# The last layer's wo products with wo moving in four column tiles, in pieces, under a newly searched order

## Chip, cores, metric

One core of one Trainium2 chip. The metric is the device time of one execution in microseconds; medians are of several executions. The record marks every run quoted here as fast: none fell in the slower state that the chip sometimes shows.

## The reference, cut to what matters

Two rounds of cached attention and an MLP over 8 sequences of one token each:

```python
W = min(4096, max(256, Sk // 4))                  # 1024 of 4096 cached positions
q = (x @ wq) in 32 heads of 128
scores = einsum(q, k[:, :, Sk - W:]) * 128 ** -0.5
o = einsum(softmax(scores), v[:, :, Sk - W:])
attention = o.reshape(B, 1, 32 * 128) @ wo        # wo: 4096 x 640
x = x + attention(layernorm(x)); x = x + mlp(layernorm(x))     # twice, same weights
```

What has to be read from memory is the caches' window and the weights; half of each sequence's cache stays in SBUF between the layers, half is read twice. In all that is 216 MB.

## The kernel before

SBUF holds the weights and 26 buffers ("units") of 4096 bytes per partition, into which SyncE's queue loads two heads of K or V at a time (512 KB, 128 rows of 4096 bytes). Every engine's instruction order comes from a searched string, ORDER. What the argument touches:

```python
P, NB, D, H, Q = 128, 8, 640, 32, 160
const = ...tile_pool(name="const"); wpool = ...; unitp = ...; state = ...   # laid out in SBUF in this order
units = [unitp.tile([P, UNIT], BF16, name=f"unit{i}") for i in range(NUNIT)]   # UNIT = 2048, NUNIT = 26
wq_sb = wpool.tile([P, NKC, H * DH], BF16, name="wq_sb")        # then wo_sb, w1_sb, w2_sb
ident = const.tile(...); ones_f = ...; nhalf = ...; ind = ...
mask_u = const.tile([P, 2], FP32, name="mask_u")
# ... (cut)
def load(which, job, i):
    s = take()                                    # a free unit, first freed first
    nc.sync.dma_start(units[s][:], cache[job.b, h0:h0 + 2, SK - W:, :].rearrange(
        "u (m c) d -> m u (c d)", c=TOK))
# ... (cut)
def gather(h0, h1):                               # last layer: heads h0 to h1 through wo, all 8 sequences
    ...
    for h in range(h0, h1):
        for n in range(NKC):                      # wo stationary, 8 columns move
            nc.tensor.matmul(a_ps[0][:, n, :], lhsT=wo_sb[:, h, n * P:(n + 1) * P], rhs=qo[:, :, h],
                             start=first, stop=(h == 2 * JOB - 1), skip_group_check=True)
            first = False
# ... (cut) the resident job's 16 heads, in one block when that job is done:
plan.add(PE, 2.2, lambda: gather(2 * JOB, H), after=[l1k[b].done], rank=1 << 20, take="att", code=160)
# ... (cut) after the searched part:
warm = units[free.pop()][:, 0:2].bitcast(FP32)
nc.scalar.activation(warm, ones_f[:], ACT.Sqrt)
nc.vector.tensor_tensor(out=xT[:, 0, 0:NKC], in0=xT[:, 0, 0:NKC], in1=a_ps[0][:], op=ALU.add)
# ... then the closing layer norm and MLP
```

The softmax here doesn't subtract the row's maximum and nothing guards it: scores larger than these inputs give would overflow.

## Time and profile before

| | before |
|---|---|
| time, median | 569.04 us (568.35 to 569.16) |
| span of the profiled run | 567.0 us |
| first transfer, last packet of the cache loads | 1.7, 547.5 us |
| closing add of the attention (xT) | 555.03 us |
| TensorE, VectorE busy | 399.2, 337.1 us |
| start of the first load buffer in SBUF | byte 117696 = 459 x 256 + 192 |

The last row is not in the profile; it is where the compiled program placed the buffer. At the time of the prediction I had not looked at it. The other rows read as follows: the loads run almost without a break to 547.5 us, and what follows is a chain of small steps. The prediction shows the lines.

### The profile page before, as it was taken

The numbers are of one execution on the slowest core, as the hardware profiler recorded it, in microseconds if no ns is written. First come the engines' busy times: TensorE is split into PE (matmuls) and PEld (weight loads), VectorE is DVE, ScalarE is ACT, GpSimd is POOL, SyncE is SP. The second block draws the span as 40 slices with busy tenths as digits, with TensorE's granted clock in tenths as the row PEclk, the third lists the DMA queues.
The fourth block names the chain that finished last, engine by engine and source line by source line (L and its number), as shares of the span: only waits on it lengthen the run. The fifth ranks groups of instructions, "written<-read, shape, count | busy, mean of one in ns | idle before, by whom it ended". The sixth has DMA issues, their size and how long they took to land.

```text
span 567.0 us, 18836 instructions
## 1 busy us (share of the span) xinstructions
PE 399.2 (70%) x8495; PEld 260.6 (46%) x8495; DVE 337.1 (59%) x665; ACT 78.0 (14%) x195; POOL 11.6 (2%) x24
## 2 busy tenths in 40 slices
PE   2303646886688778677877788777878778878985
PEld 1301434544454455355534564355635454555454
DVE  1148514695747774875568474964479474656732
ACT  0000100121011200210022001210030101210321
POOL 2000000000000000000000000000000000000000
PEclk9999655576556756755556555655575555755765
DMA  8999999999999999999999999999999999999950
GB/s 342 384 410 408 389 373 408 408 409 408 389 398 407 408 403 410 407 408 405 388 401 409 408 405 393 408 408 408 397 395 408 407 400 391 408 406 338 359 232 4
DMA packets 62758, 217.48 MB, mean 384 GB/s; under 512 B 6414, under 2 KB 12246, under 8 KB 62038
## 3 DMA queue, kind: packets, MB, share of 16 engines
q1 hardware_dynamic: 62646, 216.28, 97.2%
q8 instruction: 66, 1.08, 0.8%
q14 instruction: 14, 0.11, 0.1%
q10 hardware_dynamic: 32, 0.01, 0.0%
HBM read 216.25 MB, written 0.01 MB: 381 GB/s over the span
## 4 chain that ended last, share of the span: by engine, by line
DMA 73%; PE 19%; DVE 4%; issue 3%; SPq 1%; ACT 1%
DMA unit_97<-in_A_v_cache_dram 15%; PE s_ps L430 8%; DMA unit_111<-in_A_v_cache_dram 5%; DMA unit_103<-in_A_v_cache_dram 5%; DMA unit_87<-in_A_k_cache_dram 5%; DMA unit_107<-in_A_v_cache_dram 4%; DMA unit_103<-in_A_k_cache_dram 4%; DMA unit_95<-in_A_v_cache_dram 3%; DMA unit_100<-in_A_k_cache_dram 2%; PE qr_ps L681 2%; PE o_ps_142 L482 2%; DMA unit_112<-in_A_v_cache_dram 2%; DMA unit_109<-in_A_k_cache_dram 2%; DMA unit_87<-in_A_v_cache_dram 2%; PE o_ps_141 L482 2%
## 5 line engine op out<-in xcount | busy, mean ns | idle before, releaser
L430 PEld LDWEIGHTS <-qd_154 128*16 128x16 bf16 x512 | 14.7, 108 | 53.1 <-issue 24.1
L540 PEld LDWEIGHTS <-wo_sb 128*128 128x128 bf16 x1280 | 35.6, 103 | 7.6 <-issue 7.4
L540 PE MATMUL att<-ot,wo_sb 128*128 128x1 bf16 x1280 | 36.4, 165 | 3.1 <-DVE ot L531 1.6
L681 PE MATMUL qr_ps<-wq_sb,xn 128*32 128x512 bf16 x320 | 35.8, 609 | 0.4 <-DVE qd_154 L395 0.4
L430 PEld LDWEIGHTS <-qd_155 128*16 128x16 bf16 x512 | 15.3, 111 | 37.7 <-issue 28.6
L395 DVE CAST qd_155<-e_ps 32x64 bf16<-32x64 f32 x64 | 18.2, 285 | 15.1 <-PE e_ps L386 14.3
L430 PE MATMUL s_ps<-unit_93,qd_154 128*16 128x512 bf16 x24 | 10.8, 579 | 19.1 <-DVE qd_154 L395 19.1
L323 PEld LDWEIGHTS <-w_sb 128*128 128x128 bf16 x630 | 17.6, 104 | 10.2 <-issue 5.7
L681 PEld LDWEIGHTS <-xn 128*32 128x32 bf16 x320 | 11.8, 140 | 20.1 <-issue 16.5
L462 ACT CAST p_v<-sh_ps 128x256 bf16<-128x256 f32 x33 | 12.3, 373 | 60.7 <-PE sh_ps L455 60.6
L420 ACT COPY s_ps<-mask_u 128x512 f32<-128x512 f32 x33 | 19.5, 594 | 0.0
L395 DVE CAST qd_154<-e_ps 32x64 bf16<-32x64 f32 x64 | 18.3, 285 | 1.9 <-PE e_ps L386 1.2
L284 POOL TENSOR_TENSOR ln_w<-ln_w,nhalf 128x1 f32<-128x1 f32 x16 | 8.6, 540 | 506.7 <-DVE ln_w L276 407.1
L323 PE MATMUL h_ps<-yT,w_sb 128*128 128x1 bf16 x560 | 16.1, 165 | 4.0 <-DVE yT L289 4.0
L430 PE MATMUL s_ps<-unit_90,qd_155 128*16 128x512 bf16 x40 | 18.2, 594 | 0.8 <-DVE qd_155 L395 0.8
L356 PEld LDWEIGHTS <-w_sb 128*128 128x128 bf16 x560 | 15.8, 104 | 6.1 <-issue 1.3
L470 DVE RECIPROCAL rd<-d_ps 128x16 f32<-128x16 f32 x33 | 7.8, 238 | 18.1 <-PE d_ps L466 18.0
L414 DVE STREAM_TRANSPOSE unit_94<-unit_94 128x1024 uint32<-128x1024 uint32 x10 | 12.3, 1231 | 8.5 <-DMA unit_94<-in_A_k_cache_dram 8.4
L414 DVE STREAM_TRANSPOSE unit_92<-unit_92 128x1024 uint32<-128x1024 uint32 x10 | 12.3, 1227 | 8.4 <-DMA unit_92<-in_A_k_cache_dram 8.4
L430 PE MATMUL s_ps<-unit_108,qd_155 128*16 128x512 bf16 x36 | 16.3, 595 | 0.0
L414 DVE STREAM_TRANSPOSE unit_88<-unit_88 128x1024 uint32<-128x1024 uint32 x7 | 8.7, 1244 | 12.4 <-DMA unit_88<-in_A_k_cache_dram 12.4
L338 ACT ACTIVATE th<-hu 128x14 f32<-128x14 f32 x8 | 1.7, 215 | 104.0 <-DVE hu L333 104.0
(578 smaller groups left out, 1223.9 us busy)
## 6 DMA issues: line engine op xcount, KB each, us to landing
unit_97<-in_A_v_cache_dram SPq DMA_DIRECT2D x14, 512.0 KB, 10.3
unit_108<-in_A_k_cache_dram SPq DMA_DIRECT2D x11, 512.0 KB, 8.9
wq_sb<-in_A_wq_dram SPq DMA_DIRECT2D x5, 1024.0 KB, 9.9
wo_sb<-in_A_wo_dram SPq DMA_DIRECT2D x2, 2560.0 KB, 16.1
unit_90<-in_A_k_cache_dram SPq DMA_DIRECT2D x10, 512.0 KB, 9.2
unit_94<-in_A_k_cache_dram SPq DMA_DIRECT2D x10, 512.0 KB, 10.3
unit_100<-in_A_k_cache_dram SPq DMA_DIRECT2D x10, 512.0 KB, 10.3
unit_88<-in_A_v_cache_dram SPq DMA_DIRECT2D x10, 512.0 KB, 10.2
```

The costliest lines, as they stand in the source:

```text
L284: nc.gpsimd.tensor_tensor(out=t["wv"], in0=t["wv"], in1=nhalf[:].to_broadcast([P, nb]), op=ALU.pow)
L323: nc.tensor.matmul(t["h"][:, fc, :], lhsT=w1_sb[:, kc, c0:c0 + P], rhs=t["y"][:, kc, :], start=(kc == 0), stop=(kc == NKC - 1))
L356: nc.tensor.matmul(t["o"][:, n, :], lhsT=w2_sb[:, fc, n * P:(n + 1) * P], rhs=t["g"][:, fc, :], start=(fc == 0), stop=(fc == NFC - 1))
L395: nc.vector.tensor_copy(qd[:, :, 0:3:2, :, i], e)
L414: nc.vector.transpose(t, t)
L420: nc.scalar.copy(job.s_ps[:].rearrange("p (x u) -> p x u", u=2), mask_u[:, None, :].to_broadcast([P, 256, 2]))
L430: nc.tensor.matmul(s_ps[32 * a:32 * a + 16, :].rearrange("p (t c) -> p t c", c=32), lhsT=job.first.qd[:, je, o:o + 16], rhs=k[:, je // 2, ...
L462: nc.scalar.copy(job.p_v[:], job.sh_ps[:])
L470: nc.vector.reciprocal(job.rd[:], job.d_ps[:].rearrange("p (a z u) -> p z a u", z=2, u=2))
L482: nc.tensor.matmul(job.o_ps[:, 2 * i:2 * i + 2], lhsT=v[:, c * DH:(c + 1) * DH], rhs=job.p_v[:, a, z, c, :], start=(first and c == 0), sto ...
L540: nc.tensor.matmul(att[job.b][:, n:n + 1], lhsT=wo_sb[:, h, n * P:(n + 1) * P], rhs=job.ot[:, hi:hi + 1], start=(h == 0 and n == 0), stop= ...
L681: nc.tensor.matmul(t["qr", g][32 * a:32 * a + 32, :], lhsT=xn[:, kc, :], rhs=wq_sb[:, kc, c0:c0 + 512], start=(kc == 0), stop=(kc == NKC - ...
```

## The change

Its intent: shorten the work after the last load. The wo products of the last layer go with the 8 outputs stationary and wo moving, 320 columns at a time, four column tiles side by side, in pieces of 4 or 8 heads, so that pieces can run under the loads. The result lies as rows, in four partial sums; two copies and six fp32 matmuls against a small 0/1 matrix, sel, sum it and turn it. ORDER is searched anew for this task list.

```diff
-ORDER = ( ... )                       # all of it replaced
+ORDER = ( ... )
+    att_bank = psA.tile([P, 512], FP32, name="att")
...
+    sel = const.tile([P, 2, NB], FP32, name="sel")
+    for z in range(2):
+        nc.vector.tensor_tensor(out=sel[:, z], in0=ident[:, 32 * z:32 * z + NB], in1=ident[:, 32 * z + 64:32 * z + 64 + NB],
+                                op=ALU.add)
...
         for h in range(h0, h1):
-            for n in range(NKC):
-                nc.tensor.matmul(a_ps[0][:, n, :], lhsT=wo_sb[:, h, n * P:(n + 1) * P], rhs=qo[:, :, h], ...)
+            for z in range(2):
+                g = 64 * (h % 2) + 32 * z
+                nc.tensor.matmul(att_bank[g:g + NB, 0:2 * Q], lhsT=qo[:, :, h],
+                                 rhs=wo_sb[:, h, 2 * Q * z:2 * Q * (z + 1)], ...)
...
-        add_job(l1k[b], q2k, [normed], base=base)
-        if b + 1 == NB:
-            plan.add(PE, 2.2, lambda: gather(2 * JOB, H), after=[l1k[b].done], rank=1 << 20, take="att", code=160)
+        add_job(l1k[b], q2k, [normed], base=base, late=late if b + 1 == NB else None)
...
-    nc.vector.tensor_tensor(out=xT[:, 0, 0:NKC], in0=xT[:, 0, 0:NKC], in1=a_ps[0][:], op=ALU.add)
+    rows = units[free.pop()][:, 0:4 * Q].bitcast(FP32)
+    nc.scalar.copy(rows[:, 0:Q], att_bank[:, 0:Q])
+    nc.vector.tensor_copy(rows[:, Q:2 * Q], att_bank[:, Q:2 * Q])
+    a_ps = psC.tile([P, NKC, NB], FP32, tag="c", name="a_ps")
+    n = 0
+    while n < D:                       # 128, 128, 64, 64, 128, 128 columns
+        z, n1 = n // (2 * Q), min((n // P + 1) * P, (n // (2 * Q) + 1) * 2 * Q)
+        nc.tensor.matmul(a_ps[n % P:n % P + n1 - n, n // P, :], lhsT=rows[:, n - 2 * Q * z:n1 - 2 * Q * z],
+                         rhs=sel[:, z], start=True, stop=True)
+        n = n1
+    nc.vector.tensor_tensor(out=xT[:, 0, 0:NKC], in0=xT[:, 0, 0:NKC], in1=a_ps[:], op=ALU.add)
```

One line of it carries more than its intent: sel is 64 bytes per partition in the pool of constants, and everything laid out behind that pool, the weights and the 26 load buffers, moves up by 64 bytes.

More of the change, by code (lines that the diff above doesn't have):

```diff
@@ L45 @@
 ORDER = (
-    "57(CzL4%2#&zHzDzBz?#z@*&%)$:,#z6z:zK8-1z6zG$&zFz2z1z1+,zGzE2zAzAzBz.z.z.{){.{)z=z>z.z.z:%z~z-z8z8*-,"
-    "%zxz4z4z)z3z)+*&#z.z&z/##%$z/z%y}z.z+y}z%z*y|z%y|y|z#y~zYy|y|y|#y{zS##zQyyyyyyyyyyyy##+2$zF3ys+,zBzB"
-    "yqzAzAyq-&yoyoyoz;z;yoz:yo%(ymymymz4z6%z9z:ylz7#$yjzVz<#yjz2z;z1z/yjytyjz*yjz)&yiyiz%yoyhz)z%ynyh/%$"
-    "z#y~y|yj#yi%&(+*yty_y_z-yuybycy_yaylymy_yaz($)yhycyg#-ye*(yX#ysyWyrysyqyW$ypzXy^yny^##y[yWyZyhyhyZyT"
-    "y[yeyT&#ySzFyWyRyVyRySy[#zByRyUyUyWySySyR$yQz7#%yPyRySz2$yMz0yMyOyUyUyUyUz)$(yN%yQ$1y}$y|$/yLyyyzyyy"
@@ L51 @@
-    "LyHyK#yuyJ$ysyIyJyIypypyIyI.yH(yD&yByhyjyDyDyDyDyD&#&#yf&y=yly>yHy^y>y>y;y=y=ydyZ%yBy:y:#y[1y>y8%yZy"
-    "Wy<y7$#yPyPy9yIyNy9y5yH#&yJyeyJy6(y2$y5yA+yCyWy?yAy0y0y;y>y;y=yLy;yMy<y6,y9y9yG+yE+yF(##$y3#y(#$z%y;"
-    "y&z$#y:y%y.y$yzy+$y4y#y/y$y)y0y0y#y&y.yny#y*y%y%%y$y(y$y$&y#x}#yayay.y.y.y^y.(*+*xy#xwy&xyySy%%y$yR%"
-    "yQxzx~x~x~$x}$xyxuxsyExyxuyCxsxw%$#?.xrxrxoxq-xpxpy5xq#xpxpxmxoxoxv,xnxkxsxsy8xky9#8&3y;yU$(xlxlxzxe"
-    "y-)xlxjxj$xixsxcxry&y$%$xf$#x_xmx_xwxkxbx_(#xhxgxtxhx_#xpxhy,y)xlxmx`xg$x]xdxc$$#$x_x^xVx_xqx]xpxpxV"
@@ L56 @@
-    "x]x]xlxW(&#xXxSxSxUxUxVyLxb#$xTyIxS#x]xRxRxRxUxPxWxQ#$xT%#%xLxMxK*xMxM*xIxIxIy.y.y.xV&xUxHy*$xSy(xSx"
-    "HxGxHxPxLx}xO)xNxH&(xyxKxKxD&xIxIxsxI%xpxHxFxGxExFxjxD.CxCxC#xd#xAxB0-xKx@x@x=x?x?x<x>xDxo(x;#xkx:1$"
-    "-%x<x<x_x<#$(xWx9x3xExU.x7xCx9(+xO%$x>xexKx?x5x=xI$x4xF#x;x,x9x_xDxCx>x,xUx9x?)x2x.x<#x8x*x9x5xI#(&("
-    "x(x0x(x1x-#x@x(#x#x)x+x$x+x(x#%x3x&x2xzx3x3$#xtx#w|w~#w}x+x$x*w}x$w}%wzw|)1wywy$#x`$wuwwwuwvx[wux&x&"
-    "x&wuwux$*wvxSw~,w}xNxN&wzw{w{wx)&&wwxEwwwxxFxCxDwwwwww$0wrwtwpx;x;%#-#.#wmwm<wl0wlwlwiwe&wiwiwdwdwgw"
@@ L61 @@
-    "nwgwd#wk&wjwcwywiwbx52+wuwfx/##w^w^x(w^wow^wn-%wx&w]%wux3wxw[w^%0-wpwZwo$wnwbwowYx%x*wawlwkwawWwZw_w"
-    "U#(wT$wSw]#wYw^wXwXwnwSwowRwYwQwTwWxRwT%wSwgwcwSwbwPwa)$wPwQwPxE$%(#wMx?#&wT(wMwKwKwGwLwNx6wH$wLwL#w"
-    "HwFwFwHwHwFx+wFx*$wPwP(%$wM$wC$wzwCwywIw?wHwHwHwuwHwHwH$w>w@wFwA%#wjw<wAwhw=w@w@w@wdwC$0w>&w9w^w<w<#"
-    "0w:&)$w7w5w6w6w4w=.+#w2%w1wew7wHw7w7wYwFwV86w5w.wXw.w5w3w.wPw3wMw2w2wI)&&%,#wC$#w3w%w-w)(&w.w#w%w(w-"
-    "w6w2w+w.w%$w%w+w/)&#w@w$wFuw#$%$pqss$$ssprnw1ow3now-onw*wpnw(w(wmnw&#w%mnpmpn#$(#/ni$wZ$ggfhhfwSffr%"
@@ L66 @@
-    "qqqewM)&nnwGekwEl)kkew@w@#$&g%w<fw:fw9`^w7di^ccc$&$w.(_w,Zw+^#]Zw&w)Yw7$#)WWW`WsW^w%U],#*%vQQn$$j$h#"
-    "eik#.Pff`&(Nfcc]#%L_^GKMVGLG%$(PHODOO##LCKK$BAXCGI&TFBJIIG#AC?B$E>A@@B0#C>SSS>R#Q;>O<<M<$K+J+$H77##E"
-    "55B5A)4?4>$$?2;256$+6663#94=R40/5%131#1-0XEF#.$.-#>$==+&#%JH#8&$66%656==#&$394##$04$3.2#---.-/#%+.%*"
-    "%#()($(&##$#")
+    "zH<?1,(%zIz^)71@.3%&zC)+#)#z5#z5723+z0)zFz0z/z/zL$zHzEz0%%z@z-z,z,z,z,z?z,z,z8z8z8z,z-z~/+*z-z,*z0zx"
+    "zyz0z0zszsz0*z&&-%%$z)zkz+z$z(z##z%z&z*y|z&zez)z(y}z#y|z$y|$$y{zUyz%#zRyxyx/#2$,zMzKysysysysysys(yr-"
@@ new lines @@
+    "yqzAzAyqyqyq++yoz;z;)ynynynz7z7ynynz7ynynzHz6z7z8*%ymylz@z4z3%#z0%yi%yhyh)ygz(ygz2z,z-ymymz&z?#yl#yk"
+    "yeyeyiyiyz$yz&*ybyr#%)%yay^yoyoybyky`yj)0yjy[yhyby{y^y[#yd&%#$yVypyVyry^yVy[y[yky[yVyhyVyVyiyfyfyfzS"
+    "#zNyWyYyYyZy]yWyUy^#$yWyU%yUyT##$ySyO,yNyNyOz6yOz5z3z4yN$yMyXyOyW*z,yNyU$yTyNz&ySySyQz#z%&yQyQ$yPyP$"
+    "yHyJywyN$yIysyGyHyIyI%yHyHyl#yGyG&-+#*)yAyAy?y`y@y_y_y@y^y@y@yH,y?yZ$y>yjyby]yD&(#yay]yb4$y9y>yXy>y>"
+    "y@yU&%#*y5y;y4yNy4y7yLy7yE#y6y3y5y=yAy=yEy3y<y3yWy<y;y;y=y=,*$%%y8*yNy7y5y-#yCy.yBy2y2y2y?y?y2yAy@y?"
@@ new lines @@
+    "#/y<y2#y)y~y0z$y{$$y6y.y.##y-(y$y/%y#x~y(yly+y$y%y%$#y%x~,x{&x{x|yay`x{x}xzy)(*y&y&yVy&y&y&yT)&x}.yO"
+    "yO%#(4yLyKxzxvxyxyxy#yEyExyxxyCxxxxyAxtxwxwxw,xvy;*y<xp$y;*#y=xrxoxm*))(xlxvxl##xiy:xixgxhxhxey($y3x"
+    "dxky1y$y(#$xzy$y&xbx{xhxhxhx|x{xh#xa*%*xqxtxvxtxp#%xa+y*xbxbxZ)+xjxgxXx^#xZx{$.xaxXxa)xTxTxUxnxoxT#%"
+    "xSxX%xgxRxVxixexUxfxexUxU%xP$xOxQxRx[xXxSxRyExO#xV$&#xOxLxKxMxOy5xO$xKxJxLy2xJxJy0y.xJy-xUxUy+,xKxS%"
+    "xKxQ*y##%&xMxMxMx|xyxFxLxL*xKxt%xG%&#xoxFxFxFxFxkxFxFxFxF#xCxexBxD1#xaxaxA$*x^x=%-,x[xFx;x`x;x9x:x:x"
@@ new lines @@
+    "a$x9xax6x>xOx>,x5xL-xSxLx5x:.*(xOxMx7xfxf%%x/x/xHxbxH$$x1x-x0x-#x,x-x.*(x*x=x+xOxOx+x:x9x9xKx6x3x+x1"
+    "*))x.x.x0x0x&)#x-$%%$x&x8)x&w{x4#wz)%xww|w|wx$wzw|x+x*x%x)w}x$xiw~w}wzw|w~xdwzw}wzw|#w{.x_wxwxwux[wu"
+    "xYx%&ww&$w}(xQw|w|w|wq)wzwxxJxJ%$ww#wvwvwpwmwtwmxAws/wnwq#x<wpwpwlx8wowk%)wlwlx2wlwi#-x.x.wjx-$.)%wf"
+    "x(wpwfx(x+%we$wd&wbwbwzw`wgwawy%wew`w~wdw~w~wv$wrwcwqw^##$#wnwm$w_wjw]#wjw[wn$wiwlwhwhwZwZwVwcwewxwe"
+    "%(wTwTw`wUwX&&()(%wk$wVwh$wUwLwLwRwRwawR*wK#wOw[w]wKwJwZ&wXxBwNwWwSwLwO#wSwNwHwJ##x6wN%x4wMwHwHwEwF%"
@@ new lines @@
+    "wHx.wEwG,wDx*wD(x&%wBwMwMwDwLwFw{(wJ)w|wIw?.wGwvwtwtwtwGwEwrwF0*1(.wA(wjw@wAwhw@&#w>wdwd$wBw=wcw=w=#"
+    "w<w:wawa#w^w:w:w:w8%w8w8(w?$w4wZw5w0w2)w2wY&&w-wRw51w.w,wK%$#wJw)w)w)1wDwDw+w+wBw+w>w+w[w(w*#$(w:w3w"
+    "3w9w4w8%%vw%w/&w.w$w-+w&uw+tw<uw;w@w)w##x&($&w#vvw$pup$,$w+w+mw+w)p#ow%lw$ntprwilnrwar%m#%w[kjjk#(hh"
+    "wTwS(grfq((fwKnnnimwFwHmi&kkkccw>%dgw;(&e#b_bb$a_#w/,^w-^[],wA[$*+&*Vu(aUrTqq*SSpSSw)qlolYtw%vrYSX$#"
+    "VlmV%e#$SNeg$S$#)a`[Y,]IXLLXI&SSTS#G#Pa$E#%C#J#AJ#IGGQOGHIGBGF%EEE$DYY##EVVVDU*;AA@$OO?,MM99)&:HH:G:"
@@ L70 @@
+    "FJ7E9$C&(A84?e94:<G<@@<:8#<$8TS89()36$K4$#3&,0VUC00.,?.MM(-#,:G,*,D,%#%$$1$<0*#.##.55#+,%%#/1*$&($**"
+    "#%##%(&#$#$##")
 Q = D // 4
@@ L195, in _kernel @@
     o_banks = [psO.tile([P, 512], FP32, name=f"o_ps{i}") for i in range(2)]
+    att_bank = psA.tile([P, 512], FP32, name="att")
     for i in range(2):
-        for t in (psS.tile([P, 512], FP32, tag="s_ps", name="s_ps"), o_banks[i]):
+        for t in (psS.tile([P, 512], FP32, tag="s_ps", name="s_ps"), (o_banks + [att_bank])[i], (o_banks + [att_bank])[i + 1]):
             nc.tensor.matmul(t[:].rearrange("p (x i) -> p x i", i=P), lhsT=ident[:],
@@ L535, in project @@
         if job.p0 == 0 and h0 == 0:
-            att[job.b] = psA.tile([P, NKC], FP32, tag="att", name="att")
+            att[job.b] = att_bank[:, 0:NKC]
         for hi in range(h0, h1):
@@ L751, in _kernel @@
     free[:] = range(NUNIT)
-    a_ps = []
+    opening = [True]
     def gather(h0, h1):
-        if not a_ps:
-            a_ps.append(psA.tile([P, NKC, NB], FP32, tag="att", name="a_ps"))
-            first = True
-        else:
-            first = False
-        for h in range(h0, h1):
-            for n in range(NKC):
-                nc.tensor.matmul(a_ps[0][:, n, :], lhsT=wo_sb[:, h, n * P:(n + 1) * P], rhs=qo[:, :, h],
-                                 start=first, stop=(h == 2 * JOB - 1), skip_group_check=True)
-                first = False
+        for h in range(h0, h1):
+            for z in range(2):
+                g = 64 * (h % 2) + 32 * z
+                nc.tensor.matmul(att_bank[g:g + NB, 0:2 * Q], lhsT=qo[:, :, h],
+                                 rhs=wo_sb[:, h, 2 * Q * z:2 * Q * (z + 1)],
+                                 start=opening[0] and h < h0 + 2, stop=(h // 2 == JOB - 1), skip_group_check=True)
+        opening[0] = False
     def late(after, h0, h1):
-        return plan.add(PE, 0.14 * (h1 - h0), lambda: gather(h0, h1), after=[after], rank=1 << 20, code=10 * (h1 - h0))
+        return plan.add(PE, 0.135 * (h1 - h0), lambda: gather(h0, h1), after=[after], rank=1 << 20, code=4 * (h1 - h0))
     def add_queries(job, after=()):
```

## The prediction

> **What bounds the kernel now.** I read the page first (busy shares, the 40 slices, the chain), then the chain in order of time over the last 100 us, then a table of windows around the end, then the timeline of the last 30 us, and last the rows of the operations that the change swaps.
>
> The page says that transfers set the pace:
>
> ```profile
> PEclk9999655576556756755556555655575555755765
> DMA  8999999999999999999999999999999999999950
> ...
> HBM read 216.25 MB, written 0.01 MB: 381 GB/s over the span
> ...
> DMA 73%; PE 19%; DVE 4%; issue 3%; SPq 1%; ACT 1%
> ```
>
> The reader is to see that DMA is full in all slices but the last two, and that 73% of the chain is transfers. Where the stream is full it moves 408 GB/s; 216.3 MB at that rate are 530 us. The change removes no byte, so only two places can yield time: holes in the stream, and the tail after the stream. The windows show both (columns: stretch, its length, busy us of PE, PEld, DVE, ACT, POOL with counts, granted clock, DMA share, GB/s):
>
> ```profile
> 510.00:520.00 10.00, 9.03 (x194) 5.62 (x198) 6.89 (x17) 0.90 (x3) 0.54 (x1) 0.50 0.92 309
> 520.00:530.00 10.00, 8.19 (x161) 5.06 (x158) 6.04 (x12) 2.11 (x5) 0.54 (x1) 0.58 1.02 407
> 530.00:540.00 10.00, 8.19 (x146) 4.29 (x144) 8.65 (x17) 3.27 (x9) 0.00 (x0) 0.83 0.93 339
> 540.00:548.00 8.00, 7.18 (x160) 4.32 (x164) 2.21 (x9) 1.64 (x4) 0.00 (x0) 0.63 0.85 339
> 548.00:567.00 19.00, 12.25 (x342) 10.41 (x334) 4.79 (x23) 3.86 (x6) 0.00 (x0) 0.50 0.01 3
> ```
>
> The last load (value rows into unit_98) was issued at 537.7 and took 10.2 us, so the stream ends at 547.9. From 1.6 us, where the first transfer starts, that is 546.3 us for 530 us of bytes: some 16 us of holes, spread over the run (0 to 20 us, 510 to 520, 530 to 540 are the visible ones). The holes are waits of the load queue for TensorE and VectorE to hand a buffer back. After 547.9 come 19.1 us in which no load runs. The chain there:
>
> ```profile
> 546.77 0.59 PE o_ps_142 L482 x16
> 547.36 1.81 PE o_ps_141 L495 x16
> 549.17 0.54 PE d_ps L466 x2
> 549.71 0.40 PE o_ps_142 L482 x16
> ...
> 551.01 0.57 PE o_ps_142 L482 x16
> 551.57 0.22 PE o_ps L517 x8
> 551.79 3.22 PE a_ps L763 x120
> 555.01 0.02 issue
> 555.03 0.21 DVE xT L806
> ```
>
> From 546.8 to 555.0 TensorE is the bound and nearly never idle: values and groups that are behind the stream (about 4.9 us), then 120 of the 160 wo matmuls in one block (3.22 us). From 555.03 to 567 the closing layer norm and MLP run as one chain that the change does not touch.
>
> **What the Trainium skill says.** Four places bear on it. "TensorE: Matmul & The Clock Gate", the section "Wait — 56ns, not 53.3ns?", says that start to start never falls below about 25 ns however few columns move. The trace agrees: 120 matmuls of 8 columns in 3.22 us are 26.8 ns each at a granted clock of 0.50, and the opening's 156 of the same form took 4.24 us, 27.2 ns, at clock 1.00. So the old form costs the same at either clock. The same page, "Back-to-back issue gap", gives N/1.2 ns at the cold clock and N/2.4 warm: 320 columns would be 267 or 133 ns. The trace agrees in kind: the closing y_ps, 56 matmuls of 160 columns in four column tiles, took 2.06 us at 0.50, that is 14 rounds of 147 ns. "TensorEngine Tiling (Array Packing)", "Restrictions and Gotchas", says that column tiling excludes the fast weight load; with 8 columns of weights this costs nothing here (their load of 103 ns in the groups at L495 lies beside the matmuls). "FP8 and Floating Point Precision", "TensorE Precision Notes", counts four passes for true fp32. The trace shows two records of load and matmul for each fp32 matmul, with loads of about 0.31 us:
>
> ```profile
> L466 PE MATMUL d_ps<-rs_9825,ones_f 128*128 128x16 f32 x2 | 0.6, 386 | 0.0
> L266 PE MATMUL st_ps<-xT,ones_f 128*128 128x96 f32 x2 | 0.7, 459 | 0.6 <-DVE xT L262 0.6
> L829 PE MATMUL y_ps<-w_sb,unit_92 128*32 128x160 bf16 x56 | 2.1, 339 | 0.9 <-DVE unit_92 L345 0.9
> L763 PE MATMUL a_ps<-qo,wo_sb 128*128 128x8 bf16 x160 | 4.6, 174 | 0.0
> ```
>
> **The change part by part.** 1. *The wo products.* Before: 32 heads x 5 column blocks = 160 matmuls, wo stationary, 160 x 27 ns = 4.3 us of TensorE. After: 32 heads x 2 halves = 64 matmuls of 320 columns with the 8 queries' outputs stationary, four column tiles at a time, hence 16 rounds. At clock 0.50, which rules from 545 on, a round is 267 to 280 ns: 4.3 to 4.5 us in all; at 1.00 about 2.2 us. So at the end of this kernel the swap by itself is worth nothing; per head it is 135 ns before and 135 to 140 after.
>
> 2. *By pieces.* Before, the 16 heads of the resident job could be added only in one block after that job was wholly done (80 matmuls, 2.1 us); that block, with two late pieces of the other jobs, makes the 120 at the end. After, they go by 8 heads, each ready as soon as its half is finished. What must stay last is a piece of 4 heads: 2 rounds, the last with its latency of about 0.45 us, some 0.73 us in place of 3.35 us: 2.6 us off the path if everything else finds room earlier. There is room: between 539 and 547 TensorE stands idle for about 2 us, waiting for value loads (0.9, 0.45 and 0.55 us are the larger waits). If a piece finds no room it goes on the path at 1.1 us for 8 heads.
>
> 3. *The sum and the turn.* New on the path, after the last piece: a copy out of PSUM of 128x160 on each of two engines side by side (VectorE's copy of that size takes 0.325 us; ScalarE by the slope between its 128x256, 373 ns, and 128x512, 594 ns, about 0.29), then 6 fp32 matmuls with 128, 128, 64, 64, 128 and 128 weight columns. Each is two loads and two matmuls. In d_ps and st_ps two full loads of 0.31 us end 0.50 us after the first began, so they follow each other at 0.19 us. Eight full and four half loads: 8 x 0.19 + 4 x 0.09 = 1.9 us, plus 0.2 us until the last result. With 0.06 us of handing over the addition is 0.33 + 0.06 + 2.1 = 2.5 us. The final add of 0.20 us stays.
>
> 4. *Setup.* Two VectorE operations on 128x8 and two clearing matmuls of 512 columns, under the first weight load: nothing. The bank for att is now held for good; it had one buffer before as well: nothing.
>
> 5. *The order.* Every engine's order is another one from first load to last. This part has no cost that a row of the trace shows. It can close or open holes; 16 us are there to be had, of which the older search left these behind.
>
> Sum: tail -2.6 + 2.5, about 0; some of the 4.9 us backlog ahead of the block may move forward into idle room since the whole end was ordered afresh, which I put at -1 us (half of the 2 us idle); the holes by the new order I put at -0.5 us with a wide spread. That gives -1.5 us on 569.0: 567.5.
>
> **The rivals.** *The summation eats it and more*: if the pieces of the resident job still end up behind the stream, because its last value groups do so today (they run at 547.3 to 549.2), then 12 heads remain last: 6 rounds, 1.8 us, plus 2.5 of summation against 3.35. That makes +1 us: 570. The clock at 0.50 speaks for it. *The new order decides*: a changed sequence of buffer returns moves the stream's end by some us either way. For it speaks that all of the string changed, and that the queue's waits (single ones of up to 5 us) are many; against it, that both orders come from a search with the same aim, and that a stream 97% full has little room. It would give 563 to 572. *The swap is hidden anyway*: the tail's gain and cost cancel and the stream stays as it was: 569, same. *Faster clock*: moving matmuls of 320 columns may bring the granted clock up at the end, which would shorten the closing chain's wide matmuls by up to 1 us; but the groups at L495 (512 columns) ran at 0.50 just there, so I give it little.
>
> **How range and chances follow.** To be 2% faster the kernel would have to reach 557.7, so to find 11.3 us: two thirds of all the holes, or a tail that is more than halved. To be 2% slower it would have to lose 11.4 us, which only a bad order could do. Both get 2 in 100. The range is the order's spread about the centre: 563.5 to 571.5.
>
> **What would show it.** Right: the row of the wo products has 64 matmuls of 320 columns, the last block of them is short (under 1.3 us), two copies and about 2 us of fp32 matmuls stand between it and the add; the time from the last landing to the add shrinks from 7.1 us to 5 to 7 us; the closing chain after the add is 12 us as before; the stream ends within 4 us of 547.9. Wrong: the fp32 matmuls take under 1 us or over 3 (the loads do not follow each other at 0.19 us); the stream's end moves by more than 4 us (then the order, not the wo part, is the change); or 12 and more heads still stand at the end.

## The result, and the profile after

The changed kernel takes 556.55 us (555.75 to 557.04, 4 runs) against 569.1 us of the kernel before in the same rounds: ratio 0.978, 95% interval 0.9763 to 0.9797. Ratios here are the mean time of one kernel's fast runs over that of the other's in the same rounds, so not quite the ratio of the medians quoted. The time lies 7 us under the range that I gave.

The page of the changed kernel, the lines that answer to those in the prediction:

```profile
PEclk7555555575565655585566655675555555755775
DMA  8999999999999999999999999999999999999950
GB/s 337 416 419 409 404 395 399 396 418 417 419 414 417 418 407 406 416 418 416 406 402 418 416 408 411 416 417 417 397 417 418 417 408 414 417 393 368 367 232 4
...
HBM read 216.25 MB, written 0.01 MB: 390 GB/s over the span
...
DMA 67%; PE 22%; DVE 5%; SPq 4%; issue 1%; ACT 1%; ACTq 0%
```

And the line of the page of the kernel before that I did not print in the prediction, the rate by slice:

```profile
GB/s 342 384 410 408 389 373 408 408 409 408 389 398 407 408 403 410 407 408 405 388 401 409 408 405 393 408 408 408 397 395 408 407 400 391 408 406 338 359 232 4
```

The DMA line is the same, digit for digit. But read the rates: before, the full slices stand at 407 to 410 GB/s, and none is above. After, they stand at 416 to 419. The transfers were as busy before as after; they were slower while busy. A stretch where TensorE is all but idle shows it without any hole (columns as in the windows of the prediction). Before:

```profile
24.00:46.00 22.00, 0.60 (x3) 0.10 (x3) 11.60 (x16) 0.00 (x0) 0.00 (x0) 1.00 1.03 409
```

After:

```profile
24.00:46.00 22.00, 0.59 (x1) 0.17 (x2) 7.07 (x13) 0.00 (x0) 0.00 (x0) 0.50 1.03 420
```

TensorE has 0.6 us of work here in both, so nothing that TensorE does can explain 409 against 420 at the same DMA share of 1.03. VectorE differs, 11.60 us busy against 7.07, and the granted clock too. The first two experiments below settle that. The same stretch in before_pad64, the old order with the 64 bytes, and in after_shift, the new order without them:

```profile
24.00:46.00 22.00, 0.60 (x3) 0.18 (x4) 11.94 (x17) 0.00 (x0) 0.00 (x0) 1.00 1.03 420
24.00:46.00 22.00, 0.59 (x1) 0.18 (x2) 6.17 (x12) 0.00 (x0) 0.00 (x0) 1.00 1.03 410
```

So the rate follows neither VectorE nor the clock.

The end of the changed kernel:

```profile
530.00:535.00 5.00, 4.42 (x102) 3.10 (x100) 1.12 (x6) 1.45 (x2) 0.00 (x0) 0.84 0.82 329
535.00:554.00 19.00, 11.52 (x244) 9.50 (x244) 4.16 (x21) 2.28 (x5) 0.00 (x0) 0.50 0.01 3
```

The last packet lands at 534.9 us, 12.6 us sooner than before (547.5), and 19.1 us remain, against 19.5. So the whole gain of 13.0 us of span is in the stream except 0.4 us. Holes (stretches in which the load queue waits for a free buffer) do not explain it: before, 216.28 MB at 408 GB/s are 530.1 us of the 545.8 between first transfer and last packet, 15.7 us of holes; after, at 418 GB/s, 517.4 of 533.2, 15.8 us of holes. By these round rates, of which 1 GB/s is 1.3 us, the new order closed none of them on balance.

The chain of the changed kernel after the last loads (start, length, what):

```profile
535.33 0.58 PE o_ps_142 L487 x16
535.92 0.44 PE o_ps_141 L487 x16
...
536.60 0.99 PE o_ps_141 L487 x32
537.59 1.74 PE att L765 x19
539.33 0.02 issue
539.36 0.30 ACT unit_107 L808
539.66 0.04 issue
539.70 2.31 PE a_ps L814 x12
542.01 0.02 issue
542.03 0.21 DVE xT L817
```

From the last packet to the add it is 7.1 us, against 7.5 before: the last block is shorter (1.74 us for 3.22), and less work stands ahead of it (2.7 us for 4.3), but the copies and the fp32 matmuls (0.30 and 2.31 us) stand behind it.

The trace also holds every packet's duration. Packets of 4096 bytes are the rows of the cache loads, 49152 in each run. Of these:

| 4096-byte packets | before | after |
|---|---|---|
| mean, median | 165.0, 161 ns | 161.8, 159 ns |
| share at 160 ns or less | 45% | 98% |
| mean without the 1% of 200 ns and over | 162.1 ns | 159.1 ns |

3.2 ns on each of 49152 packets, over 16 engines, are 9.8 us; the 1280-byte and 3456-byte packets of the weights (60.3 to 57.5 and 148.6 to 135.3 ns) add 1.5, of which the 3456-byte part is mostly not the address: after_shift, with w1 where it was before, has 138.3 ns. What makes up the rest of the 12.6 us is not shown.

### The profile page after: what moved, and what is told of

Read it like the earlier page. It is cut to its first block, busy times and chain, and to the rows that moved or that the text cites. A ratio compares the mean times of both kernels' runs of the same rounds, so it can differ in the third digit from the quotient of the medians.

```text
span 554.0 us, 18686 instructions
## 1 busy us (share of the span) xinstructions
PE 400.2 (72%) x8413; PEld 260.8 (47%) x8413; DVE 335.5 (61%) x668; ACT 77.6 (14%) x196; POOL 11.6 (2%) x24
## 3 DMA queue, kind: packets, MB, share of 16 engines
q1 hardware_dynamic: 62646, 216.28, 97.5%
## 4 chain that ended last, share of the span: by engine, by line
DMA 67%; PE 22%; DVE 5%; SPq 4%; issue 1%; ACT 1%; ACTq 0%
PE s_ps L435 8%; DMA unit_104<-in_A_v_cache_dram 5%; DMA unit_112<-in_A_k_cache_dram 5%; DMA unit_96<-in_A_v_cache_dram 4%; DMA unit_91<-in_A_v_cache_dram 4%; DMA unit_89<-in_A_k_cache_dram 4%; DMA unit_94<-in_A_v_cache_dram 4%; DMA unit_94<-in_A_k_cache_dram 3%; DMA unit_89<-in_A_v_cache_dram 3%; DMA unit_99<-in_A_v_cache_dram 3%; PE o_ps_141 L487 3%; DMA unit_103<-in_A_v_cache_dram 3%; DMA unit_100<-in_A_v_cache_dram 3%; SPq L408 2%; DMA wq_sb<-in_A_wq_dram 2%; DMA unit_108<-in_A_k_cache_dram 2%
## 5 line engine op out<-in xcount | busy, mean ns | idle before, releaser
L686 PE MATMUL qr_ps<-wq_sb,xn 128*32 128x512 bf16 x320 | 33.9, 580 | 0.9 <-DVE xn L294 0.6
L435 PE MATMUL s_ps<-unit_102,qd_160 128*16 128x512 bf16 x28 | 12.5, 585 | 22.1 <-DVE unit_102 L419 22.1
L419 DVE STREAM_TRANSPOSE unit_102<-unit_102 128x1024 uint32<-128x1024 uint32 x12 | 14.8, 1231 | 15.5 <-DMA unit_102<-in_A_k_cache_dram 15.5
L328 PEld LDWEIGHTS <-w_sb 128*128 128x128 bf16 x630 | 17.5, 104 | 9.6 <-DVE yT L294 6.8
L425 ACT COPY s_ps<-mask_u 128x512 f32<-128x512 f32 x33 | 19.5, 594 | 0.1
L419 DVE STREAM_TRANSPOSE unit_109<-unit_109 128x1024 uint32<-128x1024 uint32 x11 | 13.5, 1229 | 9.4 <-DMA unit_109<-in_A_k_cache_dram 9.4
L419 DVE STREAM_TRANSPOSE unit_100<-unit_100 128x1024 uint32<-128x1024 uint32 x12 | 14.7, 1228 | 6.9 <-DMA unit_100<-in_A_k_cache_dram 6.9
L435 PE MATMUL s_ps<-unit_100,qd_161 128*16 128x512 bf16 x40 | 17.6, 580 | 0.8 <-DVE unit_100 L419 0.8
L435 PE MATMUL s_ps<-unit_94,qd_161 128*16 128x512 bf16 x40 | 18.0, 594 | 0.0
L460 PEld LDWEIGHTS <-ident 128*32 128x32 bf16 x528 | 10.1, 117 | 16.5 <-issue 14.7
L419 DVE STREAM_TRANSPOSE unit_92<-unit_92 128x1024 uint32<-128x1024 uint32 x12 | 14.8, 1231 | 5.0 <-DMA unit_92<-in_A_k_cache_dram 5.0
L435 PE MATMUL s_ps<-unit_92,qd_160 128*16 128x512 bf16 x40 | 17.1, 574 | 0.7 <-DVE hx L333 0.7
```

The costliest lines, as they stand in the source:

```text
L328: nc.tensor.matmul(t["h"][:, fc, :], lhsT=w1_sb[:, kc, c0:c0 + P], rhs=t["y"][:, kc, :], start=(kc == 0), stop=(kc == NKC - 1))
L419: nc.vector.transpose(t, t)
L425: nc.scalar.copy(job.s_ps[:].rearrange("p (x u) -> p x u", u=2), mask_u[:, None, :].to_broadcast([P, 256, 2]))
L435: nc.tensor.matmul(s_ps[32 * a:32 * a + 16, :].rearrange("p (t c) -> p t c", c=32), lhsT=job.first.qd[:, je, o:o + 16], rhs=k[:, je // 2, ...
L460: nc.tensor.matmul(job.sh_ps[32 * i:32 * i + 32, a], lhsT=ident[:, 32 * a:32 * a + 32], rhs=turned[:, :, 0:4, i].rearrange("p t (z u) -> p ...
L686: nc.tensor.matmul(t["qr", g][32 * a:32 * a + 32, :], lhsT=xn[:, kc, :], rhs=wq_sb[:, kc, c0:c0 + 512], start=(kc == 0), stop=(kc == NKC - ...
```

## The experiments

Theory A: the 64 bytes of sel moved the load buffers from 192 past a multiple of 256 bytes onto one (117696 to 117760 = 460 x 256), and that sets the packets' time. Theory B: the new order (another mix of K and V, other loads side by side) did. All runs were correct against the reference. The time of the kernel before in these calls was 568.7 to 569.2 us.

### The 64 bytes alone, and everything but the 64 bytes

The kernel before with the 64 bytes (before_pad64):

```diff
     mask_u = const.tile([P, 2], FP32, name="mask_u")
+    pad = const.tile([P, 16], FP32, name="pad")
+    nc.vector.memset(pad[:], 0.0)
```

> The kernel before with one unused constant of 64 bytes per partition ahead of the weights and the load buffers, so that the load buffers start at 117760 bytes (a multiple of 256) in place of 117696 (192 past one). Same instructions in the same order. Theory A (the start of the load buffers in SBUF sets how long a 4096-byte packet takes): nearly all packets take 159 ns, the stream ends 10 to 13 us sooner, 556 to 559 us. Theory B (the new order made the stream faster): no change, 568 to 570 us.

Measured: 557.67 us (556.04 to 557.89), ratio 0.9796 (0.9772 to 0.9820); 98.5% of the packets at 160 ns or less. Its rates by slice:

```profile
GB/s 335 391 420 418 400 397 417 417 417 419 400 403 416 419 416 411 417 419 413 400 413 419 416 410 396 419 417 418 396 409 417 417 411 403 417 416 341 341 221 4
```

The changed kernel without them (after_shift; sel lives behind the load buffers):

```diff
-    sel = const.tile([P, 2, NB], FP32, name="sel")
+    sel = state.tile([P, 2, NB], FP32, name="sel")
```

> The changed kernel with its constant sel moved behind the load buffers, so that these start at 117696 again, as in the kernel before; everything else, the order too, as changed. Theory A: packets of 161 to 169 ns come back, 567 to 570 us. Theory B: stays at 556 to 557 us.

Measured: 568.75 us (568.00 to 570.30), ratio 1.0002 (0.9994 to 1.0010); 45% of the packets at 160 ns or less. Its rates by slice:

```profile
GB/s 342 408 409 396 398 384 378 393 410 408 406 399 408 407 405 391 408 408 407 397 401 409 408 389 409 407 407 408 391 409 407 408 395 405 407 383 350 370 216 4
```

The full slices of the old order read 416 to 420 with the 64 bytes, those of the new order 407 to 410 without. Theory A holds in both directions, B falls. The 64 bytes move the weights and the tiles behind the buffers as well. These are not what counts: in the compiled after_shift the tiles behind the buffers start where they do in the changed kernel (xT at 224256 in both), and its packets are slow; in before_half, below, the weights start where they do in the kernel before, and most packets are fast.

The second run also gives the value of everything that the change meant to do: nothing, to within 0.1%. With the buffers on the grid in both it is 556.55 us (changed) against 557.67 (before_pad64); the intervals of their ratios, of four runs each, overlap, so a gain of about 1 us there is neither shown nor excluded.

### Which starts are slow

after_pad128 and after_pad32 put 128 and 32 bytes more ahead of the weights of the changed kernel (`pad = const.tile([P, 32], FP32)` and `[P, 8]`, with the same memset), before_off64 puts 128 ahead in the kernel before. after_all256 moves w1 behind the load buffers and pads 128 bytes, so that the buffers start on a multiple of 256 that is not one of 512:

```diff
+    w1pool = ctx.enter_context(tc.tile_pool(name="w1pool", bufs=1))      # right after the units' pool
-    w1_sb = wpool.tile([P, NKC, F], BF16, name="w1_sb")
+    w1_sb = w1pool.tile([P, NKC, F], BF16, name="w1_sb")
+    pad = const.tile([P, 32], FP32, name="pad"); nc.vector.memset(pad[:], 0.0)
```

> The changed kernel with 128 bytes more ahead of the load buffers: they start 128 past a multiple of 256. Theory A in its strict form (the grid is 256 bytes): packets slow again, 566 to 570 us. Theory A with a grid of 128 bytes: 556 to 557 us. Theory B: 556 to 557 us.

> The changed kernel with 32 bytes ahead of the load buffers, so that all start 32 past a multiple of 256. Any start off the grid is slow: 566 to 570 us; grid of 32 bytes: 556 to 557 us.

> The kernel before with 128 unused bytes ahead of the weights: all load buffers start 64 past a multiple of 256. If any start off the grid is slow, 566 to 570 us; if only some are (192 and 128 have been), 557 us.

> The changed kernel with w1 put behind the load buffers and 128 bytes ahead of the weights: weights and load buffers all start on multiples of 256, but the load buffers 256 past a multiple of 512. Grid of 256 bytes: packets stay at 159 ns, the weights' packets too, 555 to 556.5 us (up to 1 us under the changed kernel). Grid of 512 bytes: packets slow, 566 to 569 us.

| run | start of the load buffers past a multiple of 256 | 4096-byte packets at 160 ns or less | time, us | ratio (95%) |
|---|---|---|---|---|
| before | 192 | 45% | 569 | 1 |
| before_pad64 | 0 | 98.5% | 557.67 | 0.9796 (0.9772 to 0.9820) |
| before_off64 | 64 | 44% | 568.72 | 1.0000 (0.9992 to 1.0008) |
| after_shift | 192 | 45% | 568.75 | 1.0002 (0.9994 to 1.0010) |
| after_pad32 | 32 | 39% | 569.28 | 1.0014 (1.0004 to 1.0025) |
| after_pad128 | 128 | 59% | 566.92 | 0.9966 (0.9952 to 0.9980) |
| changed kernel | 0 | 98% | 556.55 | 0.9780 (0.9763 to 0.9797) |
| after_all256 | 0 (256 past 512) | 98% | 555.90 | 0.9774 (0.9753 to 0.9795) |

All four starts off the grid are slow, both starts on it are fast, whichever of the two orders runs. 128 past is a little less slow than the others (2 us); in that run wq, wo and w1 happen to lie on multiples of 256, so part of it may be theirs. Among the starts tried, the grid is 256 bytes, not 128 and not 512.

### How many buffers must be aligned

before_half puts the 64 bytes between the 13th and 14th load buffer of the kernel before, before_gap20 between the 20th and 21st; before_halfrev puts 64 ahead of the weights and 64 between the 13th and 14th, so that the first half is aligned and the second is 64 past.

```diff
-    units = [unitp.tile([P, UNIT], BF16, name=f"unit{i}") for i in range(NUNIT)]
+    units = [unitp.tile([P, UNIT], BF16, name=f"unit{i}") for i in range(13)]          # 20
+    gap = unitp.tile([P, 32], BF16, name="gap"); nc.vector.memset(gap[:], 0.0)
+    units += [unitp.tile([P, UNIT], BF16, name=f"unit{i}") for i in range(13, NUNIT)]  # 20
```

> The kernel before with 64 unused bytes between the 13th and the 14th load buffer: half of the buffers start 192 past a multiple of 256 as before, half on a multiple. Same order. If the start of each buffer sets the time of the packets written to it, half of the gain comes: 562 to 564.5 us, with some 72% of the 4096-byte packets at 159 to 160 ns (before 45%, all aligned 98%). If the gain came from something else that the 64 bytes shift (the weights, the state behind the buffers), it is all or nothing: 557 or 569 us.

> The reverse half: 64 bytes ahead of the weights, so that the first 13 load buffers start on multiples of 256, and 64 bytes between the 13th and 14th, so that the last 13 start 64 past one. If it is the number of misaligned loads in a row, and not which buffers or what lies behind them: as before_half, 558 to 561 us. If the second half alone matters (before_half aligned that one): 567 to 570 us.

> The kernel before with 64 unused bytes between the 20th and 21st load buffer: 20 of 26 buffers (76% of the loads) start 192 past a multiple of 256. In before_half slow packets were rare where one misaligned load followed an aligned one and common from the fifth misaligned load in a row on. Theory queue (the delay builds up over loads in a row and an aligned load lets it drain): weighted by the runs of before_half, some 20% slow packets, 560.5 to 563 us. Theory linear (each misaligned load pays for itself): 566.5 us.

Measured: before_half 559.24 us, 94% of packets at 160 ns or less; before_halfrev 558.82 us, 94% (ratio 0.9834, 0.9819 to 0.9849); before_gap20 563.81 us, 72% (0.9925, 0.9907 to 0.9943). My number for before_half was wrong: half of the alignment gave 1.7% of the 2.0% (ratio 0.9828, 0.9812 to 0.9845). So a misaligned buffer does not simply pay for itself. It is not a matter of which half, since the reverse did the same. I put the packets of these runs to their loads (128 each, in order of their starts; the loads' buffers from the same issue order in the kernel before), and took the share of packets over 160 ns by the place of a load in a row of misaligned ones:

| place in a row of misaligned loads | 1st | 2nd | 3rd | 4th | 5th |
|---|---|---|---|---|---|
| before_half | 3% | 5% | 12% | 24% | 54% |
| before_halfrev | 2% | 5% | 15% | 35% | 41% |
| before_gap20 | 8% | 18% | 38% | 48% | 52% |

So packets get slower over misaligned loads in a row, and aligned loads undo that. (The last column rests on 3, 4 and 25 loads.) The number that I drew from this for before_gap20 (560.5 to 563) was too low and the linear one (566.5) too high: with only 6 aligned buffers the recovery is not complete, as the first column shows (8% where before_half had 3%). That some queue on the write side fills and drains is my reading; no row of the trace shows a queue.

### What the moving form costs, and what the rest is worth

The changed kernel with the old form of the products, in the new pieces and order, added directly (after_oldform):

```diff
-            for z in range(2):
-                g = 64 * (h % 2) + 32 * z
-                nc.tensor.matmul(att_bank[g:g + NB, 0:2 * Q], lhsT=qo[:, :, h], rhs=wo_sb[:, h, 2 * Q * z:2 * Q * (z + 1)], ...)
+            for n in range(NKC):
+                nc.tensor.matmul(att_bank[:, n * NB:(n + 1) * NB], lhsT=wo_sb[:, h, n * P:(n + 1) * P], rhs=qo[:, :, h], ...)
...
-    rows = ...                          # the two copies and the six fp32 matmuls
-    ...
-    ... in1=a_ps[:], op=ALU.add)
+    ... in1=att_bank[:, 0:NKC * NB].rearrange("p (k b) -> p k b", b=NB), op=ALU.add)
```

> The changed kernel (its order, its pieces, its buffer addresses) with the old form of the wo products, five matmuls of 8 columns a head with wo stationary, added at once without the copies and the fp32 matmuls. If the sum and turn are a plain addition to the path (0.34 us of copies and 2.3 us of matmuls in the trace of the changed kernel) and the two forms cost alike per head, it is 2 to 3 us faster than the changed kernel: 553.5 to 554.5 us. If the moving form earned something (clock, fewer instructions) that pays for it, it is equal or slower: 556 us or more.

Measured: 556.78 us (555.42 to 557.53), ratio 0.9787 (0.9766 to 0.9808): no gain, as the rival said. But its timeline of ScalarE at the end shows an accident:

```profile
542.40 0.21 ACT L286 ACTIVATE unit<-unit 128x8 f32<-128x8 f32 x1 [3.83 <-DVE unit L281]
546.42 1.28 ACT L343 ACT_TABLE_LOAD   x1 [3.81 <-DVE unit L338]
547.71 0.30 ACT L343 ACTIVATE unit<-unit 128x112 f32<-128x112 f32 x1
```

The load of the table for tanh waits for VectorE and then stands on the path with 1.28 us. In the changed kernel it ran at 544.28, right after the square root. Without the buffer `rows`, the later buffers of the end are other ones. In the compiled program the table load and the activation carry one wait each: in the changed kernel the table load has one for a transfer long done and the activation the one for VectorE; in after_oldform the table load has the one for VectorE, and the activation one for ScalarE's own earlier use of its output buffer. One more line, `free.pop()` ahead of eye, takes the same buffers as the changed kernel does (after_oldform2).

> As after_oldform, with the later buffers of the end taken as in the changed kernel, so that the load of ScalarE's table for tanh no longer waits for VectorE (in after_oldform it came at 546.4 in place of about 542.6 and put 1.3 us on the path). Theory: the sum and turn cost 2.6 us and nothing pays for them: 554 to 555 us. Rival (the moving form pays for its sum): 556 to 557 us.

Measured: 554.14 us (553.94 to 555.48), ratio 0.9745 (0.9727 to 0.9763). That is 2.6 us under after_oldform in the medians and 1.1 us in the profiled spans (552.5 against 553.6), where the table load explains 1.28; what the rest is, scatter of four runs or not, is not shown. Its ScalarE and its chain:

```profile
542.69 0.21 ACT L286 ACTIVATE unit<-unit 128x8 f32<-128x8 f32 x1 [3.83 <-DVE unit L281]
542.92 1.28 ACT L343 ACT_TABLE_LOAD   x1
```

```profile
539.03 1.62 PE att L764 x60
540.65 0.02 issue
540.68 0.21 DVE xT L805
```

The block of 12 heads takes 1.62 us in the old form and 1.74 in the moving form; then the add follows at once. From last packet to add it is 4.4 us (536.3 to 540.7) against 7.1 in the changed kernel. So the sum and turn is a plain loss of some 2.4 us in the medians (about 2 us by the ratios, 0.978 against 0.9745, which come from different calls and whose intervals just touch), and no run shows the moving form paying for any of it.

Both together, old form and everything on multiples of 256 (best):

> after_oldform2 and after_all256 together: the old form of the wo products in pieces in the new order, all weights and load buffers on multiples of 256. If both gains are real and add: 553 to 554.5 us, faster than both kernels.

Measured: 554.09 us (553.20 to 554.82), ratio 0.9738 (0.9720 to 0.9757). It beats both kernels. That the weights' alignment adds anything to after_oldform2 is not shown: the intervals overlap almost wholly, although the 1280-byte packets went from 57.4 to 55.3 ns.

## Why the prediction was wrong

**The step that failed** is part 4, "Setup: ... nothing". It weighed what building sel costs in instructions and did not ask where its 64 bytes lie. With the address put back, all the rest of the change is worth 0.0% (after_shift); with the address alone, the kernel before becomes 2.0% faster (before_pad64). The same error sat in the first section, in "only two places can yield time": the third is the rate itself. I took 408 GB/s "where the stream is full" as the floor and 530 us as what the bytes need. It was the rate of misaligned writes; aligned ones move 418, and the floor is 517 us. A busy share of 1.03 could not tell the two apart, for it says that the engines always have a packet in hand, not how long each takes. The Trainium skill's "DMA: Bandwidth & Descriptors", section "How a descriptor splits into AXI transactions", would have raised the question: it says that a transaction must start from a 256-byte boundary, so that a descriptor that starts off one has its first transaction at the boundary below. The page speaks of reading; to carry it over to writes into SBUF is my step. The runs agree on the grid of 256. By that rule I estimate 17 transactions for a row of 4096 bytes off the grid in place of 16, or 6% more; the rate fell by 2.4%, so the count alone does not give the cost.

**Point by point.**

- *The wo products*: 64 matmuls of 320 columns as said; the rule of equal cost per head nearly held (1.74 against 1.62 us for 12 heads). (The prediction left out the 2.5 ns that "Back-to-back issue gap" adds to the warm figure; nothing rests on it.)
- *By pieces*: half wrong. I expected 4 heads to remain last and the block to stay under 1.3 us; 12 remained (24 matmuls, 1.74 us), one of my own signs of being wrong. The first rival had that number, but not its reason: the resident job's pieces did run under the loads (40 matmuls, for 20 heads, from 532.0 us on), and what stayed are three pieces of 4 heads of the streamed jobs, whose outputs VectorE wrote only from 536.4, 536.5 and 537.6 us on.
- *The sum and turn*: 2.31 us of matmuls where I had 2.1, and 0.30 of copies on the chain where I had 0.33; the sizes were right, the overlap was not. The two copies did not run side by side: VectorE's waited for ScalarE's and ran from 539.68 to 540.00, beside the first fp32 matmuls, which hid it.
- *Tail*: predicted 5 to 7 us from the last landing to the add; by the landing (535.3 us, a little after the last packet's end) it is 6.7, within. That is partly luck: the block saved 1.5 us where I had 2.6, what follows it costs 2.7 from the block's end to the add where I had 2.5, and the backlog ahead of the block shrank by 1.6 (4.3 to 2.7 us) where I had 1.
- *The order*: I gave -0.5 us (and 5 us for the longest waits of the load queue, where its record has one of 7.2); the holes stayed (15.7 and 15.8 us), and after_shift, whose tail is 7.2 us but whose last packet lands 0.4 us later than before, leaves nothing for tail and order together.
- *Faster clock*: the last stretch ran at 0.50 as before.
- *The criterion for being wrong*, that the stream's end moves by more than 4 us, was met (12.6 us); but the conclusion that I had tied to it, "then the order", was wrong too. I had no rival in which the packets themselves change.

## What to carry to other kernels

When transfers bound a kernel, print where the destination buffers start in SBUF, and put them on multiples of 256 bytes; here 64 idle bytes were worth 11 us, where undoing the sum and turn was worth 2.4. Compare the rate of the full slices and the packets' durations between versions before crediting an order or an algorithm, and when a change adds any tile, put the addresses back once and measure. A form of matmul that costs the same per head has to earn the passes that it adds behind it, and on the path to the end these did not.

## What the Trainium skill lacked or had wrong

- "DMA: Bandwidth & Descriptors", "How a descriptor splits into AXI transactions": it gives the 256-byte rule, worded for reads, without saying what it costs a stream of large rows into SBUF. Here: 159.1 ns a packet of 4096 bytes on the grid, 162.1 off it (packets under 200 ns), 418 against 408 GB/s.
- The same place counts beats, by which, if it holds for writes too, I estimate 130 for a row that starts at 64 and 134 for one at 192, against 128. The runs show no difference between the two: before_off64 takes 1.0000 (0.9992 to 1.0008) of the kernel before, at 568.72 us each.
- No page that I found says that the cost of misaligned rows grows over loads in a row: 3% slow packets in the first load of a row of misaligned ones, 54% in the fifth (before_half); aligning 13 of 26 buffers gave 1.7% of the 2.0% that all of them give.
- No page that I found says that a wait can fall on the load of an activation table in place of the activation, so that the choice of an output buffer puts 1.28 us on the path (after_oldform).
